# A finer cost model for the instruction order, a split z chain, TensorE flips and more GLU tiles in the FFT stage

## The chip, the cores and the metric

The kernel runs on one core of one Trainium2 chip. The metric is the device time of one execution in microseconds (us), the median of several. A run counts as slow when it is over 1.5% above the fastest run of the same kernel; fast runs are compared with fast runs. The engines are named as in the profile: PE is TensorE (PEld its weight loads), DVE is VectorE, ACT is ScalarE, POOL is GpSimd, SP is the sync engine, which here only issues transfers.

## The reference

The kernel computes a gated block and all its gradients: one output and nine gradients. S = 2048, D = 512, F = 1376, bf16.

```python
# cut: inputs, random numbers and casts are left out
def _A_ref(q, k, v, shift_k, ssm_k, ssm_D):        # q is xn
    k_shift = ...                                   # causal 4-tap filter of k along the sequence
    kv = k_shift * v
    # causal convolution along the sequence by FFTs of length 2 S:
    y = irfft(rfft(pad(kv)) * rfft(pad(ssm_k)))[:S]
    y = y + kv * ssm_D
    return q * y

def _B_ref(x, w_gate, w_up, w_down):                # the GLU
    h = sigmoid(x @ w_gate) * (x @ w_up)
    return h @ w_down

x = A_q
xn = layernorm(x)
s = _A_ref(xn, A_k, A_v, A_shift_k, A_ssm_k, A_ssm_D)
g = silu(_B_ref(xn, B_w_gate, B_w_up, B_w_down))
out = x + s * g
# the kernel returns out and the vector-Jacobian product with grad_out for nine inputs
```

## The kernel before

The FFTs are matmuls with constant matrices. Four stages follow each other: the start (loads, constants), the FFT stage (forward convolution, beside it the forward GLU of eight of the sixteen tiles, of which five are spilled to DRAM), stage B (GLU backward tile by tile, and the forward of the other tiles), and stage C (backward FFT and weight gradients).

The program does not issue its instructions in the order in which it is written. It records them with their dependences, and a scheduler, with a model of each instruction's cost, simulates the engines and puts the instructions of each engine in the order of that simulation. So a wrong cost in the model is a wrong order on the chip. The parts that matter here:

```python
def cost(self, alt):                       # (time on the engine, time to the result)
    if eng == "scalar":
        c = 0.085 + n / 1200
        return c, c + 0.11
    ...                                    # other engines
# cut: in the simulation, when op (started at t, engine occupied for occ, result at fin) is placed
    o = ops[s]                             # an op that depends on it
    r = t + occ if (e == "tensor" and o.alts[0][0] == "tensor") or (e == o.alts[0][0] \
        and len(o.alts) == 1 and not op.dma) else fin + 0.05
    o.ready = max(o.ready, r)              # same engine: ready as soon as the engine is free
```

```python
FA = [12, 10, 8, 6, 4, 0, 1, 2]            # tiles whose forward runs in the FFT stage

def z_gen(i):                              # down projection and gates of tile i, in stage B
    nc.vector.tensor_tensor(s_out, xn, y2, ALU.mult)
    nc.vector.tensor_tensor(dgate, goj, s_out, ALU.mult)
    for fb in range(NFB):
        nc.tensor.matmul(psZ[:], hT[:, fb, :], wd[:, fb, :], ...)
        if fb == 5:
            yield 6 * 512
    # sigmoid on ScalarE, then a chain of dependent VectorE products up to dzA[:, i, :]
    ...
    yield 5 * 512
    # the rest of the chain

def stepB():
    for i in range(NJ):
        ...                                # f: forward of tile i+3, d: dh, x: dx of tile i
        yield from take(z, 9)              # all of z of tile i+1, before most of d
        ...
        yield from take(d, 9); yield from take(f, 9); yield from take(x, 9)

def flip_dma(Qg, Qf):                      # stage C: transposes by transfers on the sync queue
    for c in range(2):
        nc.sync.dma_start_transpose(Qf[:, c], Qg[:, c].rearrange("p g j e -> p (g j e)"))
# stage C, in the gradient of the 4-tap filter:
    nc.vector.memset(dks[96:P, NJ:NJ + 3, :], 0.0)
```

Of the kernel before, what the change touches and what calls it, by code (L numbers as in the profile page):

```python
# [30 lines left out]
FA = [12, 10, 8, 6, 4, 0, 1, 2]  # L31
# [121 lines left out]
class Op:  # L153
    __slots__ = ("n", "alts", "deps", "succ", "wait", "ready", "dma", "tiles", "done", "fin", "eng", "soft")
# [12 lines left out]
class Rec:  # L167
# [64 lines left out]
    def add(self, alts):  # L232
# [37 lines left out]
        op.dma = "dma" in meth  # L270
        self.ops.append(op)
# [8 lines left out]
    def cost(self, alt):  # L280
# [7 lines left out]
        if eng == "scalar":  # L288
            c = 0.085 + n / 1200
            return c, c + 0.11  # L290
        if eng == "vector":
            aps = [v for v in list(a) + list(k.values()) if isinstance(v, (PT, bass.AP))]
            big = [v for v in aps if self.size(v) >= n / 2]
            ps = any(isinstance(v, PT) for v in big)
            wide = any(esize(v.ap.dtype if isinstance(v, PT) else v.dtype) == 4 for v in big)
            rate = 960
            if meth in ("tensor_copy", "tensor_scalar", "tensor_single_scalar", "tensor_scalar_add", "memset"):
                rate = 1920 if (wide and not ps) or (ps and not wide) else 960 if ps else 3840
            elif meth == "tensor_tensor" and not ps and not wide:
                rate = 1920  # L300
            if meth == "bn_stats":
                n = self.size(a[1])
            c = 0.065 + n / rate
            return c, c + 0.09
        if "alu" in meth or meth == "tensor_tensor":
            return 0.3, 1.5
# [27 lines left out]
    def order(self):  # L334
# [30 lines left out]
        seq = []  # L365

        def push(op):
            if len(op.alts) > 1:
                either.append(op)
            else:  # L370
                heapq.heappush(soon[op.alts[0][0]], (op.ready, op.n))
# [13 lines left out]
        while ndone < len(ops):  # L385
# [58 lines left out]
            ndone += 1  # L444
            for v in op.tiles:
# [12 lines left out]
            for s in op.succ:  # L458
# [7 lines left out]
                r = t + occ if (e == "tensor" and o.alts[0][0] == "tensor") or (e == o.alts[0][0] and len(o.alts) == 1 and not op.dma) else fin + 0.05  # L466
# [42 lines left out]
def gen_fft_consts(nc, ar, negpi, Cf, BD, R):  # L509
# [8 lines left out]
    a = tmp([16], i32)  # L518
    nc.gpsimd.iota(a, pattern=[[1, 16]], base=0, channel_multiplier=16)
    b = tmp([128], i32)  # L520
    nc.gpsimd.iota(b, pattern=[[2, 128]], base=1, channel_multiplier=0)
# [50 lines left out]
def kernel_impl(ctx, tc, A_q, A_k, A_v, A_shift_k, A_ssm_k, A_ssm_D, B_x, B_w_gate, B_w_up, B_w_down,  # L572
# [97 lines left out]
    def f_gen(i):  # L670
# [3 lines left out]
        xnT = xnT_r.next()  # L674
        nc.evac(xnT, pt[:], 512)
        yield 512
        n = POS[i]
        if n + 3 < NJ:
            f_x(SEQ[n + 3])
        sigT, hT = sig_r.next(), h_r.next()  # L680
        T[i]["sig"], T[i]["h"] = sigT, hT
        for pi, (f0, nb) in enumerate(FBS):
# [11 lines left out]
            nc.vector.tensor_tensor(hT[:, f0:f0 + nb, :], pu[:, 0:nb, :], sigT[:, f0:f0 + nb, :], ALU.mult)  # L694
            if pi == 1 and n + 1 < NJ:
                f_ln(SEQ[n + 1])
            yield nb * 1024
# [50 lines left out]

    skr_r = Ring(ar, [D * 4])
    ones_r = Ring(ar, [P])  # L750
    skr, ones1 = skr_r.ap[0:1, :], ones_r.ap[0:1, :]
    nc.sync.dma_start(skr, A_shift_k.rearrange("(o d) t -> o (d t)", o=1))
    for i in SEQ[:3]:
# [3 lines left out]
    def ld_w(f0, f1):  # L757
        for w, src in ((wg, B_w_gate), (wu, B_w_up)):
            nc.sync.dma_start(w[:, :, f0:f1], src[:, f0:f1].rearrange("(db p) f -> p db f", p=P))
    ld_w(0, 512)  # L760
    ld_k(0)
    ld_KT(0)
    ld_w(512, 1024)
    ld_w(1024, F)
    ld_v(0)
    nc.scalar.dma_start(Dcol_b, A_ssm_D.rearrange("(cg p) -> p cg", p=P))
    stS_r.append(Ring(ar, [FP]))
# [9 lines left out]
    for db in range(4):  # L777
        pb = ps_mm([512])
        nc.tensor.matmul(pb[:], ones1, skr[:, db * 512:(db + 1) * 512], start=True, stop=True)
        nc.scalar.copy(skb[:, :, db * 128:(db + 1) * 128], pb[:].rearrange("p (d t) -> p t d", t=4))  # L780
    nc.gpsimd.memset(wg[:, :, F:FP], 0.0)
    nc.gpsimd.memset(wu[:, :, F:FP], 0.0)
    make_identity(nc, ident)
    f_ln(SEQ[0])
    gen_fft_consts(nc, ar, negpi, Cf, BD, R)
# [39 lines left out]

    def flip_dma(Qg, Qf):
        for c in range(2):
            nc.sync.dma_start_transpose(Qf[:, c], Qg[:, c].rearrange("p g j e -> p (g j e)"))
# [40 lines left out]
    def strK():  # L869
        for cg in range(NG):  # L870
            KT = stA.pop(("KT", cg))
            nc.gpsimd.tensor_tensor(out=KT[:, 0:1], in0=KT[:, 0:1], in1=Dcol_b[:, cg:cg + 1], op=ALU.add)
# [80 lines left out]
    run_streams([(gG, len(FA) * 11776, 0.1, 0.97), (strK(), 4 * 10240, 0.0, 0.7), (strV(), 4 * 16384, 0.0, 0.8),  # L953
# [24 lines left out]
    dg_r, du_r = Ring(ar, [NFB, 128], n=2), Ring(ar, [NFB, 128], n=2)  # L978

# [29 lines left out]
    def z_gen(i):  # L1009
# [5 lines left out]
        nc.vector.tensor_tensor(s_out, xn, y2, ALU.mult)  # L1015
        nc.vector.tensor_tensor(dgate, goj, s_out, ALU.mult)
# [9 lines left out]
        nc.scalar.activation(t2, sigz, ACT.Identity, bias=1.0, scale=-1.0)  # L1026
        nc.vector.tensor_tensor(t2, gate, t2, ALU.mult)
        nc.vector.tensor_tensor(t2, t2, sigz, ALU.add)
        nc.vector.tensor_tensor(dzA[:, i, :], dgate, t2, ALU.mult)
        yield 5 * 512  # L1030
# [56 lines left out]
    def stepB():  # L1087
        yield from z_gen(0)
        for i in range(NJ):
# [11 lines left out]
            yield from take(f, 1)  # L1101
            run_pend(2)
            yield from take(z, 9)
            if i == NJ - 2:
                flags.add("z15")
# [10 lines left out]
            yield from take(f, 9)  # L1116
            run_pend(2)
            yield from take(x, 9)
            if i + LAG == NJ - 1:
# [60 lines left out]
    def frontC():  # L1180
        for cg in range(NG):
# [5 lines left out]
            flip_dma(Qg, Qf)  # L1187
# [14 lines left out]
    def backC():  # L1202
        for cg in range(NG):
# [33 lines left out]
            nc.vector.memset(dks[96:P, NJ:NJ + 3, :], 0.0)  # L1237
# [92 lines left out]
    live = run_streams([(dw[0], dw[1] - dw[4], 0.0, 1.0), (frontC(), 4 * 4096, -0.05, 0.5),  # L1330
# [67 lines left out]
```

## Time and profile before

| | before |
|---|---|
| timed runs | 604.84 us median of 3 (603.37 to 610.57) |
| profiled run | 597.06 us, span 595.3 us |
| TensorE busy | 540.4 us, 91% |
| sum of its matmuls back to back | 521.4 us |

The last row is the floor that I use below. Unbroken runs of matmuls start 55.8 ns (128 columns) and 215.8 ns (512 columns) apart; I put N/2.4 GHz + 2.5 ns on each of the 5261 matmuls, of which every weight load is in the trace. The time from the first matmul to the last (by the starts of their weight loads) less this floor is what I call waits of TensorE: idle time and half-clock time together, 67.1 us before. A half-clock spell is a stretch in which the clock record shows half the full clock.

The prediction shows the main views of this kernel. Two more lines of its page are needed for comparison: the granted clock of TensorE in 40 slices (in tenths, 9 is full), and the shares of the engines in the chain of waits that ended last.

```profile
PEclk9989999999999999999999999989999999999998
PE 33%; DVE 23%; DMA 18%; issue 17%; ACT 4%; POOL 4%; POOLq 0%; DVEq 0%; ACTq 0%
```

The clock drops in three slices. By the clock record these are the spells at 39.1 and 394.1 us and a fourth one at 592.1 us, which begins after the last matmul has ended (589.8 us) and costs nothing; the spell at 489.7 us falls on the border of two slices and does not show. TensorE has only a third of the chain; 18% is transfers and 23% VectorE. The next view is the timeline of VectorE in stage B (start, duration, then engine, operation and shapes), the statistics of one layer norm tile:

```profile
210.43 0.69 DVE L479 BATCH_NORM_STATS2 slab<-slab 128x6 f32<-128x512 bf16 x1
211.16 0.18 DVE L479 BATCH_NORM_AGGREGATE slab<-slab 128x2 f32<-128x6 f32 x1
211.37 0.15 DVE L479 TENSOR_SCALAR slab<-slab 128x1 f32<-128x1 f32 x1
```

Each step needs the one before, and each starts only after the record of the one before has ended: 210.43 + 0.69 = 211.12, start 211.16. I counted all neighbours on VectorE in this trace. 277 start 20 to 60 ns after the end of their predecessor's record, and 274 of these wait on VectorE's own semaphore; 500 start before that end, 83 ns in the median. In the products of 128x512 bf16, the two kinds show as starts 0.456 us (80 times) and 0.336 us (216 times) apart. A dependent neighbour costs 0.12 us more.

### The profile page before, as it was taken

Reading aid. Unit: us, or ns where it says so; the run is one execution under the profiler, and the core shown is the slowest. Engines: PE = TensorE matmul, PEld = TensorE weight load, DVE = VectorE, ACT = ScalarE, POOL = GpSimd, SP = SyncE. Lnnn points to the kernel's source line nnn. Section 1 sums busy time; section 2 is a strip of 40 time slices with the busy share of each in tenths; the row PEclk is TensorE's granted clock in tenths of the full one; section 3 lists DMA queues with packets and bytes.
Section 4 is the critical chain, followed back from the end, with each engine's and each line's share of the span. In section 5 each row is a group of like instructions: output and inputs, shape, how many; then the busy total and the mean of one; then the engine's idle time right before and its main releaser. Section 6 shows DMA issues by size and latency. Waiting matters only on the chain.

```text
span 595.3 us, 12849 instructions
## 1 busy us (share of the span) xinstructions
PE 540.4 (91%) x5197; PEld 372.0 (62%) x5261; DVE 436.8 (73%) x874; ACT 327.2 (55%) x437; POOL 151.0 (25%) x258
## 2 busy tenths in 40 slices
PE   4878899999989889899889989969999989999986
PEld 3866678787876556566667656534665645665534
DVE  7699998683878887889878789422859688479350
ACT  7879999797853434354334334224646655444411
POOL 2332242422011312222112111310323152340211
PEclk9989999999999999999999999989999999999998
DMA  8976888665217676989876799999899979985561
GB/s 228 276 197 187 272 210 219 203 212 152 89 53 198 173 210 152 242 165 239 195 223 183 174 209 284 216 195 294 228 229 283 217 245 283 217 261 194 150 185 34
DMA packets 143367, 121.64 MB, mean 204 GB/s; under 512 B 91508, under 2 KB 124106, under 8 KB 143307
## 3 DMA queue, kind: packets, MB, share of 16 engines
q1 hardware_dynamic: 126362, 67.03, 47.2%
q0 software_dynamic: 16416, 53.78, 30.3%
q8 instruction: 41, 0.67, 0.5%
q14 instruction: 20, 0.16, 0.1%
q10 hardware_dynamic: 528, 0.00, 0.0%
HBM read 52.79 MB, written 46.11 MB: 166 GB/s over the span
## 4 chain that ended last, share of the span: by engine, by line
PE 33%; DVE 23%; DMA 18%; issue 17%; ACT 4%; POOL 4%; POOLq 0%; DVEq 0%; ACTq 0%
PE psum L479 33%; DVE slab L479 23%; DMA slab<-slab 8%; ACT slab L479 4%; DMA out_dram<-slab 2%; DMA KK_d<-slab 2%; DMA slab<-in_grad_out_dram 2%; POOL slab L479 1%; DMA ksh_d<-slab 1%; DMA hF_d<-slab 1%; POOL out_dram L479 1%; POOL KK_d L479 1%; DMA slab<-in_A_k_dram 1%; POOL sF_d L479 0%; POOLq L479 0%
## 5 line engine op out<-in xcount | busy, mean ns | idle before, releaser
L479 PE MATMUL psum<-slab 128*128 128x128 bf16 (+4 forms) x5197 | 540.4, 263 | 49.4 <-ACT slab L479 25.5
L479 PEld LDWEIGHTS <-slab 128*128 128x128 bf16 (+2 forms) x5261 | 372.0, 99 | 217.5 <-issue 36.4
L479 DVE TENSOR_TENSOR slab<-slab 128x512 bf16<-128x512 bf16 (+5 forms) x551 | 301.4, 587 | 39.9 <-ACT slab L479 23.2
L479 ACT CAST slab<-psum 128x1024 bf16<-128x1024 f32 (+4 forms) x245 | 201.5, 855 | 159.7 <-PE psum L479 135.3
L479 POOL DMA_DIRECT2D out_dram<-slab x75 | 44.1, 591 | 219.7 <-DVE slab L479 141.0
L479 ACT COPY slab<-psum 128x1024 bf16<-128x1024 bf16 (+2 forms) x74 | 60.5, 839 | 27.9 <-PE psum L479 27.5
L479 DVE TENSOR_TENSOR slab<-psum,slab 128x512 bf16<-128x512 f32 (+2 forms) x68 | 44.4, 655 | 27.0 <-PE psum L479 15.1
L479 ACT ACTIVATE slab<-psum 128x512 bf16<-128x512 f32 (+1 forms) x64 | 37.3, 584 | 48.8 <-PE psum L479 46.1
L479 ACT ACTIVATE slab<-slab 128x512 bf16<-128x512 bf16 (+3 forms) x51 | 40.2, 802 | 25.6 <-DVE slab L479 24.9
L479 POOL DMA_DIRECT2D KK_d<-slab x32 | 20.2, 637 | 48.2 <-ACT slab L479 39.3
L479 DVE SCALAR_TENSOR_TENSOR slab<-slab 128x1 f32<-128x1 f32 (+3 forms) x64 | 28.0, 438 | 4.0 <-ACT slab L479 2.8
L479 DVE CAST slab<-psum 128x1024 bf16<-128x1024 f32 (+1 forms) x12 | 14.1, 1177 | 19.4 <-PE psum L479 18.8
L479 POOL DMA_DIRECT2D slab<-in_A_q_dram x29 | 16.5, 570 | 37.5 <-ACT slab L479 21.7
L479 DVE COPY slab<-psum 128x1024 bf16<-128x1024 bf16 (+2 forms) x26 | 16.1, 632 | 12.8 <-PE psum L479 12.6
L479 DVE SCALAR_TENSOR_TENSOR slab<-psum,slab 128x512 f32<-128x512 f32 x16 | 11.0, 690 | 18.9 <-PE psum L479 18.8
L479 POOL DMA_DIRECT2D slab<-KK_d x16 | 11.6, 723 | 29.2 <-DVE slab L479 27.1
L479 DVE TENSOR_SCALAR slab<-slab 128x1 f32<-128x1 f32 (+8 forms) x49 | 16.8, 358 | 1.7 <-ACT slab L479 1.0
L479 POOL TENSOR_TENSOR slab<-slab 128x1 f32<-128x1 f32 (+1 forms) x20 | 12.9, 646 | 12.3 <-DVE slab L479 10.7
L479 POOL DMA_DIRECT2D slab<-in_grad_out_dram x16 | 9.3, 579 | 16.7 <-DMA out_dram<-slab 15.3
L479 DVE BATCH_NORM_STATS2 slab<-slab 128x6 f32<-128x512 bf16 x16 | 11.0, 688 | 0.6 <-DMA slab<-in_A_q_dram 0.5
L479 POOL DMA_DIRECT2D slab<-slab x8 | 4.6, 572 | 24.7 <-DVE slab L479 16.5
L479 POOL DMA_DIRECT2D slab<-in_A_k_dram x12 | 10.2, 851 | 1.5 <-issue 0.7
(22 smaller groups left out, 39.3 us busy)
## 6 DMA issues: line engine op xcount, KB each, us to landing
KK_d<-slab POOLq DMA_DIRECT2D x32, 256.0 KB, 3.9
slab<-KK_d POOLq DMA_DIRECT2D x16, 512.0 KB, 7.5
out_dram<-slab POOLq DMA_DIRECT2D x58, 128.0 KB, 4.0
hS_d<-slab SPq DMA_DIRECT2D x16, 352.0 KB, 3.0
dgS_d<-slab SPq DMA_DIRECT2D x16, 352.0 KB, 3.3
duS_d<-slab SPq DMA_DIRECT2D x16, 352.0 KB, 3.6
slab<-hS_d SPq DMA_DIRECT2D x8, 512.0 KB, 5.0
slab<-dgS_d SPq DMA_DIRECT2D x8, 512.0 KB, 8.1
```

The lines of the kernel that those rows point to most:

```text
L479: getattr(getattr(self.nc, eng), meth)(*[place(v) for v in a], **{x: place(v) for x, v in k.items()})
```

## The change

It has these parts: a finer model for the order; the z chain of the next tile split, so that its last part stands after the matmuls of d and x of this tile; two more buffers for it; the flips of dy in stage C as TensorE transposes; layer norm two tiles ahead and the transposed tile (xnT) one tile ahead; another load order; ten forward tiles in the FFT stage instead of eight, seven of them spilled instead of five; and one memset from VectorE to GpSimd. (Also one small addition from GpSimd to VectorE, and new weights of the streams.) The core of the diff:

```diff
-FA = [12, 10, 8, 6, 4, 0, 1, 2]
+LATE = 0.25
+AHEAD = 500
+FA = [14, 13, 11, 9, 7, 5, 4, 0, 1, 2]
@@ model: durations
-            c = 0.085 + n / 1200
-            return c, c + 0.11
+            c = 0.05 + n / 1200 + (0.2 if not isinstance(k.get("scale", 1.0), float) else 0.0)
+            return c, c + 0.12
... (VectorE 0.065 to 0.07; reductions by their input; GpSimd scalar operations)
@@ model: transfers that are far ahead of TensorE are held back
+            if op.dma and op.n > front[0] + AHEAD:
+                held.append(op)
@@ model: latency
-                r = t + occ if (e == "tensor" and o.alts[0][0] == "tensor") or (... same engine ...) else fin + 0.05
+                same = e == o.alts[0][0] and len(o.alts) == 1 and not op.dma
+                r = t + occ + (0.0 if e == "tensor" else 0.12) if same else fin + 0.05 + (LATE * (fin - t) if op.dma else 0.0)
@@ z_gen: three parts instead of two
-        nc.vector.tensor_tensor(s_out, xn, y2, ALU.mult)
-        nc.vector.tensor_tensor(dgate, goj, s_out, ALU.mult)
...
+        yield 5 * 512
+        nc.vector.tensor_tensor(s_out, xn, y2, ALU.mult)
         nc.vector.tensor_tensor(t2, gate, t2, ALU.mult)
+        nc.vector.tensor_tensor(dgate, goj, s_out, ALU.mult)
...
-        yield 5 * 512
+        yield 64
@@ stepB
-            yield from take(z, 9)
+            yield from take(z, 2)
...
             yield from take(f, 9)
+            yield from take(z, 1)
             run_pend(2)
             yield from take(x, 9)
+            yield from take(z, 9)
@@ stage C
-            flip_dma(Qg, Qf)
+            yield from flip(Qg, Qf)
...
-            nc.vector.memset(dks[96:P, NJ:NJ + 3, :], 0.0)
+            nc.gpsimd.memset(dks[96:P, NJ:NJ + 3, :], 0.0)
... (layer norm and xnT ahead, load order, buffers: left out)
```

## The prediction

> **What bounds the kernel now.** I read the page first. Its first part says that TensorE (PE) holds the span:
>
> ```profile
> span 595.3 us, 12849 instructions
> PE 540.4 (91%) x5197; PEld 372.0 (62%) x5261; DVE 436.8 (73%) x874; ACT 327.2 (55%) x437; POOL 151.0 (25%) x258
> ```
>
> So TensorE is idle for 595.3 - 540.4 = 54.9 us, and busy time can shrink only if work is removed. Next, the waits of TensorE: whom it waits for in its idle time.
>
> ```profile
> PE psum L479 <- ACT slab L479: 25.5, 28, 5.1
> PE psum L479 <- DVE slab L479: 16.8, 21, 4.4
> ...
> PE psum L479 <- DMA slab<-slab: 0.6, 1, 0.6
> ```
>
> 42.3 us are waits for the two engines that empty PSUM and prepare operands; transfers are almost never what TensorE waits for directly. Third, the busy times in stretches that I cut by the program's stages, found from what is stored and loaded when (spills of h and KK_d stores in the first part, dgS_d stores in the middle, KK_d loads and output stores at the end): start, FFT stage, stage B (GLU backward), stage C (backward FFT and weight gradients).
>
> ```profile
> core 0: us, PE busy (x) PEld busy (x) DVE busy (x) ACT busy (x) POOL busy (x), PEclk, DMA share, GB/s
> 0.00:28.00 28.00, 17.75 (x229) 15.47 (x230) 19.81 (x53) 23.63 (x27) 8.33 (x25) 1.00 0.92 261
> 28.00:166.00 138.00, 127.31 (x1630) 105.47 (x1647) 113.42 (x182) 121.22 (x145) 40.51 (x67) 0.99 0.67 189
> 166.00:398.00 232.00, 211.02 (x2076) 141.31 (x2097) 185.28 (x452) 90.14 (x156) 48.33 (x85) 0.99 0.81 196
> 398.00:596.00 198.00, 184.32 (x1270) 109.71 (x1290) 118.30 (x188) 92.21 (x110) 53.83 (x83) 0.98 0.80 216
> ```
>
> Length less PE busy gives the idle time of each stage: 10.3, 10.7, 21.0 and 13.7 us (0.7 of the last lies past the end). In the FFT stage ScalarE (ACT) is busy 88% and VectorE (DVE) 82%, so three engines are near full there. In stage B DVE has 80% and ACT 39%.
>
> Last, the timeline at two stalls of stage B. The first repeats whenever a GLU forward tile runs inside this stage:
>
> ```profile
> 215.65 1.05 ACT L479 CAST slab<-psum 128x512 bf16<-128x512 f32 x2
> 216.59 0.59 ACT L479 COPY slab<-psum 128x512 bf16<-128x512 bf16 x1
> 217.24 0.55 PE L479 MATMUL psum<-slab 128*128 128x128 bf16 x7 [1.48 <-ACT slab L479]
> ```
>
> TensorE has just transposed a normalised tile; the copy to SBUF (bf16 from bf16 PSUM, so a transpose) stands behind two other evictions on ACT, and the first gate matmul waits 1.48 us. The second is the border of B and C:
>
> ```profile
> 393.18 0.22 DVE L479 MEMSET slab<- 32x192 uint32 x1 [11.07 <-DMA slab<-slab]
> ...
> 394.18 2.29 PE L479 MATMUL psum<-slab 128*128 128x512 bf16 x5 [4.36 <-DVE slab L479]
> 394.18 0.10 PEld L479 LDWEIGHTS <-slab 128*128 128x128 bf16 x1 [4.48 <-issue]
> 394.56 0.15 PEld L479 LDWEIGHTS <-slab 128*128 128x128 bf16 x1 [0.28 <-issue]
> 394.99 0.15 PEld L479 LDWEIGHTS <-slab 128*128 128x128 bf16 x1 [0.28 <-issue]
> ```
>
> A DVE memset of a stage C buffer waits 11.07 us for a transfer (transposing reads of the memory it reuses), the last tile's arithmetic queues behind it, and TensorE waits 4.36 us for the PSUM bank that this arithmetic reads. Then the weight loads come 0.43 us apart, twice the usual spacing.
>
> **What the skill says.** "TensorE: Matmul & The Clock Gate", section "Wait — 56ns, not 53.3ns?", gives N/2.4 GHz + about 2.5 ns between starts, 55.6 and 215.7 ns for 128 and 512 columns. The trace agrees: unbroken runs start 55.8 and 215.8 ns apart. Part 1 of the page gives half clock after an idle window of about 3.4 us. The trace's clock record has three such spells inside the span, 3.41 us each, at 39.1, 394.1 and 489.7 us; a spell costs up to 1.7 us. Its "Engine queue depths" says that ACT and DVE are strict FIFO; the memset shows it. Its "Part 4: PE-mode transpose" says that a transpose lands in PSUM and needs a copy, about 275 ns each in a kernel; here a 128-column record lasts 221 ns on average, but their starts are 55.8 ns apart, so I cost 55.8.
>
> **The change, part by part.**
>
> *dy flips on TensorE.* Four groups, each 2 x 16 transposes: 128 x 55.8 ns = 7.1 us more on TensorE, all in stage C where it is 93% busy, so all on the path. 16 evictions at 1.04 us (row ACT COPY 128x1024) = 16.6 us of ACT, which has 106 us free in C: beside. Eight transfers of 512 KB leave the sync queue, and with them waits such as 372.88 to 403 us in the chain, which holds "DMA slab<-slab" pieces of 20.2 and 9.5 us. But TensorE fills stage C with weight-gradient matmuls (14.92 of 15 us busy from 405 to 420), so the earlier start of the backward FFT is worth little by itself.
>
> *Two more tiles in the FFT stage.* A tile is 92 matmuls of 128 columns = 5.13 us. So 10.3 us of TensorE work move from B to the FFT stage; the sum is unchanged. ACT takes per tile two sigmoids of 512 (0.61) and one of 384 (0.51), the xnT copy (0.59) and the LN activation (0.73) = 3.05 us; DVE takes 2 x 0.69 + 0.55 + LN 1.2 = 3.1 us. Two spills and reloads more are 2 x 2 x 352 KB each way, 2.8 MB, some 10 us of transfer at 270 GB/s (an estimate from the rates in the stretches), beside.
>
> *xnT and LN ahead.* Stalls over 1 us in B: about 1.5, 1.7, 1.7, 1.7, 1.2, 1.5, 1.2, 1.0, 2.0 and the 4.4 at the border, some 18 of 21 us. Four stand directly behind an xnT copy; the others are a PSUM bank or operand that waits for ACT or DVE while those stand behind something that came too early. Taking xnT a tile ahead removes the four, 6.5 us.
>
> *z chain split and finer model.* z of the next tile now starts before the matmuls of d and x of this one, so its ten DVE steps have about 7 us (44 x 55.8 ns + 22 x 215.8 ns) to hide in. With the finer order I give them half of the remaining 7 us: 3.5.
>
> *Memset to GpSimd.* The DVE queue is free at the border: 4.4 us and the half-clock spell (up to 1.7): 6.
>
> *Load order and start.* One x tile before the weights, K's filter before k, LN before the FFT constants: first tile matmul at 9.16 us now. I give 3 of the 10.3 us.
>
> Sum by stage. Start and FFT stage: 166 now; + 10.3 work, - 3 start, - 3 idle filled by the extra tiles (10.7 us is there, but ACT at 88% limits it) = 170. B: 232 - 10.3 - 6.5 - 3.5 - 6 = 205.7; I add 3 for the ten tiles without forward work (before eight), where DVE's 11.3 us per tile exceeds TensorE's 9.8 = 209. C: 197.3 + 7.1 - 2 (fewer waits for transfers) = 202. Total 581. Taking the reverse way, the idle time falls from 55 to about 32 and busy time rises by 5 (7 less a half-clock spell): 577. I take 579, a ratio of 0.973. The timed median is 604.84, above the profile's 595.3, so 604.84 x 0.973 = 588; I lean to 586, as the reordering touches more small waits than I counted.
>
> **Rivals.** (1) *The FFT stage takes it all back.* Before: ACT + DVE of start and FFT stage 278 us over two engines, 139 of 166 us. After: 278 + 12.3 = 290, 145 us, and TensorE 155. If packing stays as it is, the stage grows by the whole 10.3, and the start gives nothing: +6, about 592. For it: 88% ACT. Against: late in the stage (135 to 150 us) DVE has 6 and ACT 10.7 of 15 us, and the new weights of the streams put the tiles earlier, where TensorE has 11 to 13 of 15.
> (2) *DVE becomes the bound of B.* DVE 185 - 2 x 3.1 = 179 us in B against TensorE's 201. At the 80% of now that is 224 us, so B would shrink by only 8: total near 594 profiled, 604 timed, no gain. Against: DVE's own idle time in B is mostly waiting for TensorE and ACT.
> (3) *The flips cost more than they free.* If C was hidden behind weight gradients anyway, +7 and no return: 2 us more than I count.
> (4) *All idle of B vanishes.* Then B is 201, total 570, timed 575.
>
> **Range and chances.** Point 586. Rivals (1) and (2) in part give 598; (4) with a better FFT stage gives 572. Timed runs scatter between 603.4 and 610.6. Faster by over 2% (below 592.7): 0.73; within: 0.23; slower: 0.04.
>
> **What would show it.** PE busy near 545; idle near 32. No 1.5 us stall behind a 512-wide bf16 copy in B. No 11 us DVE memset wait, and one half-clock spell fewer. First tile matmul near 7 us. End of the FFT stage near 170, of B near 379. 48 instead of 56 DMA transposes, ACT COPY 128x1024 up by about 16. It is wrong if the FFT stage ends past 178, if DVE is over 92% in B, or if the memset now blocks GpSimd's queue of transfers so that stage C waits for loads.

## The result

The changed kernel takes 566.41 us (median of 4 runs, 564.35 to 569.34, all fast); the kernel before takes 605.57 us beside it (4 runs). The ratio is 0.9346, 95% interval 0.9268 to 0.9425. A ratio is taken within one job, from runs of the same rounds, so it is not quite the ratio of the medians. The result lies below the predicted range of 572 to 598 us: faster, as expected, but by about twice the predicted gain.

From the page of the changed kernel, and its waits of TensorE (engine, what it wrote, whom it waited for: us in all, times, longest):

```profile
span 562.7 us, 13136 instructions
PE 536.1 (95%) x5330; PEld 378.2 (67%) x5389; DVE 420.8 (75%) x873; ACT 343.1 (61%) x454; POOL 155.2 (28%) x266
```

```profile
PE psum L493 <- ACT slab L493: 13.0, 14, 5.2
...
PE psum L493 <- DVE slab L493: 2.2, 4, 1.0
```

Waits for ScalarE fall from 25.5 to 13.0 us, and waits for VectorE from 16.8 us in 21 pieces to 2.2 us in 4. The window view by stage, cut as in the prediction some 5 to 10 us behind the ends of the stages that the table of waits below gives:

```profile
core 0: us, PE busy (x) PEld busy (x) DVE busy (x) ACT busy (x) POOL busy (x), PEclk, DMA share, GB/s
0.00:28.00 28.00, 19.27 (x223) 15.86 (x225) 18.55 (x49) 22.91 (x26) 6.45 (x20) 1.00 0.87 246
28.00:176.00 148.00, 138.95 (x1912) 120.04 (x1926) 121.96 (x209) 130.87 (x165) 47.18 (x80) 1.00 0.72 204
176.00:372.00 196.00, 193.70 (x1847) 127.79 (x1864) 167.18 (x432) 85.42 (x144) 47.30 (x84) 1.00 0.98 229
372.00:564.00 192.00, 184.15 (x1358) 114.54 (x1379) 113.10 (x185) 103.87 (x122) 54.24 (x84) 1.00 0.66 200
```

In stage B TensorE is idle for 2.3 of 196 us, where it was idle for 21.0 of 232 us. DVE has 85% there and is not the bound. Most of the idle time left is in the first two rows. The clock and the chain answer to the two lines shown of before:

```profile
PEclk9999999999999999999999999999999999999999
PE 64%; DVE 14%; issue 9%; ACT 9%; POOL 2%; DMA 1%; POOLq 0%; DVEq 0%; ACTq 0%
```

All three half-clock spells that lay between matmuls are gone, and the share of transfers in the chain falls from 18% to 1%. VectorE in stage B, where the same three statistics instructions run (208 to 212 us):

```profile
209.04 0.68 DVE L493 BATCH_NORM_STATS2 slab<-slab 128x6 f32<-128x512 bf16 x1
209.65 0.67 DVE L493 SCALAR_TENSOR_TENSOR slab<-psum,slab 128x512 f32<-128x512 f32 x1
...
211.19 0.17 DVE L493 BATCH_NORM_AGGREGATE slab<-slab 128x2 f32<-128x6 f32 x1
211.31 0.16 DVE L493 SCALAR_TENSOR_TENSOR slab<-slab 128x2 f32<-128x2 f32 x1
211.40 0.15 DVE L493 TENSOR_SCALAR slab<-slab 128x1 f32<-128x1 f32 x1
```

Work of other chains now stands between the dependent steps, and each instruction starts before the record in front of it has ended (209.65 against 209.04 + 0.68 = 209.72). Dependent neighbours on VectorE fall from 277 to 98. At 0.12 us each that is 21 us; VectorE's busy time, with nearly the same instructions, falls by 16.0 us (436.8 to 420.8).

The waits by stage, by the floor method. The cuts are at 28 us, at the last matmul of the FFT streams, at the last matmul of dx in stage B, and at the end:

| | floor | start | FFT stage (ends) | stage B (ends) | stage C | all waits |
|---|---|---|---|---|---|---|
| before | 521.4 | 13.5 | 17.2 (160.4) | 19.1 (386.4) | 17.3 | 67.1 |
| after | 528.5 | 11.9 | 12.7 (170.8) | 2.0 (362.0) | 0.9 | 27.5 |

The floor grows by 7.1 us, waits fall by 39.6, and the span by 32.6. The timed medians differ by more, 39.2 us: the profiled run of before (597.06 us) was some 8 us faster than its median, that of after (564.47) some 2 us.

### The profile page after: what moved, and what is told of

Same layout as the page of the kernel before. It is cut to its first block, busy times and chain, and to the rows that moved or that the text cites. A ratio compares the mean times of both kernels' runs of the same rounds, so it can differ in the third digit from the quotient of the medians.

```text
span 562.7 us, 13136 instructions
## 1 busy us (share of the span) xinstructions
PE 536.1 (95%) x5330; PEld 378.2 (67%) x5389; DVE 420.8 (75%) x873; ACT 343.1 (61%) x454; POOL 155.2 (28%) x266
## 4 chain that ended last, share of the span: by engine, by line
PE 64%; DVE 14%; issue 9%; ACT 9%; POOL 2%; DMA 1%; POOLq 0%; DVEq 0%; ACTq 0%
PE psum L493 64%; DVE slab L493 14%; ACT slab L493 9%; POOL out_dram L493 1%; DMA ksh_d<-slab 1%; POOL slab L493 0%; POOLq L1420 0%; POOLq L493 0%; DVEq L493 0%; ACTq L493 0%; POOLq L1409 0%
## 5 line engine op out<-in xcount | busy, mean ns | idle before, releaser
L493 PE MATMUL psum<-slab 128*128 128x128 bf16 (+4 forms) x5330 | 536.1, 261 | 21.3 <-ACT slab L493 13.0
L493 PEld LDWEIGHTS <-slab 128*128 128x128 bf16 (+1 forms) x5389 | 378.2, 99 | 178.8 <-issue 13.3
L493 DVE TENSOR_TENSOR slab<-slab 128x512 bf16<-128x512 bf16 (+3 forms) x555 | 291.5, 579 | 38.4 <-ACT slab L493 25.3
L493 ACT CAST slab<-psum 128x1024 bf16<-128x1024 f32 (+3 forms) x242 | 200.1, 857 | 98.9 <-PE psum L493 92.7
L493 ACT COPY slab<-psum 128x1024 bf16<-128x1024 bf16 (+2 forms) x94 | 79.4, 887 | 86.9 <-PE psum L493 86.3
L493 DVE SCALAR_TENSOR_TENSOR slab<-slab 128x1 f32<-128x1 f32 (+3 forms) x64 | 28.0, 437 | 13.8 <-ACT slab L493 12.6
L493 DVE COPY slab<-psum 128x1024 bf16<-128x1024 bf16 (+2 forms) x22 | 14.0, 646 | 19.9 <-PE psum L493 18.4
L493 DVE CAST slab<-psum 128x1024 bf16<-128x1024 f32 (+1 forms) x15 | 17.4, 1161 | 9.0 <-PE psum L493 8.9
L493 DVE TENSOR_SCALAR slab<-slab 128x1 f32<-128x1 f32 (+8 forms) x49 | 16.6, 355 | 2.0 <-ACT slab L493 1.8
L493 POOL TENSOR_TENSOR slab<-slab 128x1 f32<-128x1 f32 x16 | 11.4, 712 | 18.3 <-DVE slab L493 18.1
L493 POOL DMA_DIRECT2D slab<-slab x8 | 4.5, 566 | 26.0 <-issue 17.1
L493 DVE BATCH_NORM_STATS2 slab<-slab 128x6 f32<-128x512 bf16 x16 | 10.8, 683 | 0.0
```

Source lines behind the costliest of these rows:

```text
L493: getattr(getattr(self.nc, eng), meth)(*[place(v) for v in a], **{x: place(v) for x, v in k.items()})
```

## The experiments

Each run was made beside the kernel before on the same chip. That kernel's medians in the five jobs were 602.32, 604.07, 600.29, 607.22 and 602.34 us, slow runs included; its fast runs alone give 602.32, 604.06, 598.75, 601.18 and 596.58 us. In the fourth job (after_no012, after_noLate, before_LZT, before_ZT) four of the seven runs of the kernel before count as slow, and the ratios come out only with these left in: against its three fast runs (mean 600.99 us) I get 0.974, 0.954, 0.977 and 1.019. The changed kernel itself ran only in the first job; times are compared across jobs. Four versions that change little (after_noMem, after_mc, after_noG, after_11) took 566.4 to 567.3 us on three chips, so its 566.41 us carries over. The runs of one kernel lie up to some 6 us apart, except where the table says more, so differences below that are not settled by a median. Waits are from the profiled run, by stage as above; for the kernels without the new flips the floor is 521.4 us, for the others 528.5; the profiled run of after_noM is a slow one. "Dependent" is the number of dependent neighbours on VectorE, where I counted it.

| kernel | timed median (range), us | ratio to before (95%) | waits start / FFT / B / C | dependent |
|---|---|---|---|---|
| before | 605.57 (603.37-610.57) | 1 | 13.5 / 17.2 / 19.1 / 17.3 | 277 |
| after | 566.41 (564.35-569.34) | 0.935 (0.927-0.943) | 11.9 / 12.7 / 2.0 / 0.9 | 98 |
| after_noM | 619.11 (605.29-627.57) | none | 15.9 / 29.0 / 16.5 / 29.2 | 256 |
| after_noZ | 592.76 (589.32-597.53) | 0.984 (0.977-0.992) | 12.1 / 12.6 / 28.0 / 1.0 | 99 |
| after_noT | 572.47 (569.52-574.53) | 0.949 (0.943-0.956) | 12.5 / 12.5 / 1.9 / 16.6 | 103 |
| before_M | 611.36 (609.39-614.89) | 1.015 (1.009-1.021) | 14.9 / 12.7 / 22.0 / 25.4 | 89 |
| after_noX | 577.10 (569.47-578.65) | 0.951 (0.938-0.964) | 11.4 / 17.2 / 2.9 / 1.2 | |
| after_noMem | 566.66 (564.91-570.86) | 0.942 (0.934-0.949) | 12.7 / 12.6 / 1.9 / 0.9 | |
| after_noF | 571.61 (569.21-576.64) | 0.951 (0.941-0.961) | 12.4 / 15.9 / 1.4 / 4.3 | |
| after_noHold | 568.38 (565.50-573.26) | 0.944 (0.936-0.953) | 12.4 / 14.4 / 1.4 / 2.8 | |
| after_noConst | 568.99 (565.67-571.13) | 0.950 (0.945-0.956) | 13.1 / 9.5 / 2.8 / 6.4 | 99 |
| after_noLat | 589.84 (588.87-591.32) | 0.985 (0.981-0.990) | 15.4 / 17.8 / 13.1 / 7.5 | 263 |
| before_MZT | 571.37 (568.90-573.70) | 0.955 (0.950-0.960) | 14.5 / 13.8 / 2.7 / 0.9 | 115 |
| after_mc | 567.18 (565.11-570.90) | 0.948 (0.943-0.954) | 10.6 / 12.9 / 1.9 / 8.5 | |
| after_no012 | 585.08 (583.67-586.67) | 0.967 (0.959-0.975) | 12.8 / 20.2 / 10.8 / 2.9 | 264 |
| after_noLate | 578.01 (569.15-580.60) | 0.946 (0.933-0.959) | 12.0 / 12.5 / 2.0 / 5.6 | 92 |
| before_LZT | 586.97 (585.73-587.95) | 0.969 (0.963-0.975) | 14.3 / 13.6 / 14.0 / 8.6 | 111 |
| before_ZT | 611.95 (611.08-613.77) | 1.011 (1.004-1.017) | 13.5 / 17.5 / 16.4 / 27.0 | 264 |
| after_noG | 567.27 (565.69-570.87) | 0.951 (0.942-0.960) | 11.5 / 12.0 / 4.8 / 1.4 | |
| after_11 | 566.43 (562.01-572.12) | 0.952 (0.939-0.965) | 11.5 / 10.7 / 1.9 / 1.1 | |

### One large part undone or done alone

**after_noM.** All changes of the model undone (durations, hold-back, latency), the rest of the change kept.

```diff
-            c = 0.05 + n / 1200 + (0.2 if ... else 0.0)
+            c = 0.085 + n / 1200
... and the other lines of the model, as in the kernel before
```

> The changed kernel with the old cost model for the order (old constants, no holding back of transfers, no added latency between instructions of one engine), all else as changed. Theory A, the finer model places the work and took away most waits of TensorE in stages B and C (34 of the 40 us gained): time near 590, 20 us or more of TensorE waits back in B and C. Theory B, the restructuring (xnT ahead, z split, flips, memset) took them away and the model only trims: under 575, waits in B and C together under 8 us.

Three of its four runs, the profiled one among them, count as slow, so there is no ratio, and the 619 us mixes states. Its one fast run took 605.29 us. That alone says enough: with everything else of the change in place and the old model, the kernel is about where it was before. Theory B fails; theory A has the place right (stages B and C) and the size too small.

**after_noZ.** The z chain is issued as before.

```diff
-            yield from take(z, 2)
+            yield from take(z, 9)
... z_gen in two parts, its first two products ahead of the matmuls
```

> The changed kernel with the z chain as before (one piece, all of it ahead of the matmuls of d and x, s_out and dgate first). Theory B (structure): the z chain stands in VectorE's queue ahead of what TensorE needs, 8 to 12 us of waits come back in stage B, time near 576. Theory A (model): the order is found anyway, at most 3 us, under 570.

It is 26.3 us slower by the medians, and all of it is in stage B, whose waits go from 2.0 to 28.0 us. The timeline of TensorE there, with the idle time before a piece in brackets:

```profile
247.62 1.05 PE L493 MATMUL psum<-slab 128*128 128x128 bf16 x16 [0.93 <-ACT slab L493]
249.36 1.28 PE L493 MATMUL psum<-slab 128*128 128x128 bf16 x20 [0.69 <-ACT slab L493]
251.08 23.08 PE L493 MATMUL psum<-slab 128*128 128x128 bf16 x215 [0.45 <-ACT slab L493]
275.09 1.05 PE L493 MATMUL psum<-slab 128*128 128x128 bf16 x16 [0.93 <-ACT slab L493]
```

The same three gaps, 0.93, 0.69 and 0.45 us, return every 27.5 us, once per round of the order. They are small, and none looks like a 26 us problem; over the stage, with some longer ones, they are one. In all, TensorE waits in stage B 11.9 us for ScalarE in 18 pieces and 7.9 us for VectorE in 4, against 0.8 us each in the changed kernel; two half-clock spells come on top. Each of the three short gaps waits for a ScalarE instruction on a result that TensorE has only just made (in the first, at 247.00 us, it stands behind two activations of z); the two longest, 2.89 and 2.69 us, end with a 128x512 product of VectorE. That the unsplit chain leaves TensorE no other matmuls at these places is my reading. Dependent neighbours stay at 99, so the model's part still works. Theory B had the direction, with a third to a half of the size; theory A fails.

**after_noT.** The flips of dy are transposing transfers again.

```diff
-            yield from flip(Qg, Qf)
+            flip_dma(Qg, Qf)
```

> The changed kernel with dy flipped by DMA transposes again: 7.1 us less matmul time. My prediction's reading (stage C is full of weight-gradient matmuls, the flips only cost): 559 to 562, faster than the changed kernel by 4 to 7 us. Rival, the transposes hold up the sync queue and with it the loads and the start of the backward FFT: C gets 7 us or more of waits back, time 566 to 572.

The floor falls by 7.1 us as it must, but the waits of stage C rise from 0.9 to 16.6: the profiled span is 8.7 us longer, the median 6.1. The timeline of TensorE in stage C:

```profile
412.72 27.44 PE L493 MATMUL psum<-slab 128*128 128x512 bf16 x202 [2.80 <-DMA slab<-slab]
444.57 1.67 PE L493 MATMUL psum<-slab 128*128 128x256 bf16 x6 [4.41 <-DVE slab L493]
```

"DMA slab<-slab" at 412.72 us is one of the flips: issued at 396.57 us, it landed at 412.68. Only this gap waits for a flip directly. At 444.57 us TensorE waits for VectorE work that had itself waited 4.96 us for a transfer of GpSimd's queue, and a third gap, 2.90 us before 471.52, stands behind ScalarE, which had waited 4.03 us for an output store. That these two come from the later start of the backward FFT is my reading. The clock record has half-clock spells of 3.41 us at 413.3, 444.0 and 471.3 us, within 0.6 us of the ends of these three gaps. So the 7.1 us of transposes buy back about 16 us of waits, of which up to 5.1 us are half clock. My prediction's reading (559 to 562 us) fails; its rival holds, though the time is just above its 566 to 572 us and only one gap is the queue's directly.

**before_M.** The kernel before with the finer model alone.

```diff
... only the lines of the model of the change
```

> The kernel before with only the finer cost model. Theory A: 580 to 585 (20 us or more of waits in B and C gone). Theory B: 598 to 606, waits in B still over 18 us.

It is 1.5% slower than before; theory A fails, and the time lies above theory B's range too. Dependent neighbours fall to 89, so the rule does what it is for; the waits of stage B stay (22.0 us) and those of stage C grow to 25.4. Its waits of TensorE say on what:

```profile
PE psum L492 <- ACT slab L492: 25.5, 32, 5.1
PE psum L492 <- DMA slab<-slab: 14.3, 2, 7.5
PE psum L492 <- DVE slab L492: 10.7, 6, 3.8
```

Two waits of about 7 us, before 411.83 and 539.94 us, are for the flips by transfer. The order is better packed, and the two things that the program itself forces, the unsplit z chain and the flips on the sync queue, stay. (That the waits of stage B are owed to the z chain is inferred: before_MZT, with the split, has 2.7 us there.)

### The smaller parts

**after_noX.** Layer norm and xnT are made just in time, as before.

```diff
-    def f_xnT(i): ...
... xnT back in f_gen, f_ln(SEQ[n + 1]) back
```

> The changed kernel with xnT and the layer norm just in time again (one tile ahead for LN, xnT at the start of its own tile), z split and the rest kept. My prediction gave this part 6.5 us in stage B (four stalls behind an xnT copy, now six tiles run there). If it stands: 6 to 10 us of waits back in B, time 573 to 577. Rival, with z out of the way the copy comes in time anyway: under 3 us, under 570.

The profile shows 5.2 us more waits, of which 4.5 are in the FFT stage (12.7 to 17.2) and 0.9 in stage B. Only two of its four timed runs count as fast (569.47 and 576.13 us), so the time says no more than "some us". The expected 6 to 10 us of waits in stage B did not come.

**after_noMem.** The memset stays on VectorE.

```diff
-            nc.gpsimd.memset(dks[96:P, NJ:NJ + 3, :], 0.0)
+            nc.vector.memset(dks[96:P, NJ:NJ + 3, :], 0.0)
```

> The changed kernel with the memset of the stage C buffer on VectorE again. My prediction gave it 6 us at the border (4.4 us wait and a half-clock spell). If it stands: TensorE waits 4 us or more at the end of B and the time is 571 to 573. Rival: the wait came from the DMA transposes of dy in front of the sync queue and from the late z chain; with those gone the memset finds its memory free, under 1 us, 565 to 568.

Nothing changes: 566.66 us. The memset at the border of stages B and C, in the timeline of VectorE:

```profile
358.96 0.22 DVE L493 MEMSET slab<- 32x192 uint32 x1 [0.55 <-DMA slab<-slab]
```

It waits 0.55 us where it waited 11.07 us before. With the rest of the change its wait has gone already, so it no longer matters on which engine it stands. The rival's time holds; its reason, the flips in front of the sync queue, does not, as shown below.

**after_noF.** Eight forward tiles in the FFT stage, as before.

```diff
-FA = [14, 13, 11, 9, 7, 5, 4, 0, 1, 2]
+FA = [12, 10, 8, 6, 4, 0, 1, 2]
```

> The changed kernel with eight forward tiles in the FFT stage instead of ten (old list, five spilled). The sum of matmul time stays. If the FFT stage had idle TensorE time for the two tiles (my prediction gave 3 us): 568 to 572, FFT stage ending near 163. Rival: the two tiles only move their 10.3 us and B has as little waiting either way: within 2 us of the changed kernel.

5.2 us slower by the medians and 6.2 us longer in the profile. Stage B has no more waits than after (1.4 us); the FFT stage has 3.2 more and stage C 3.4 more. In the FFT stage the two tiles fill idle time; why stage C differs I did not trace.

### Which line of the model

**after_noHold.** Transfers are not held back.

```diff
-AHEAD = 500
+AHEAD = 1000000
```

> The changed kernel with the cost model's new constants but without holding transfers back until the matmul front is within 500 operations of them. The old model as a whole cost 60 us. If the hold is what counts (transfers placed far too early block their queue): 580 or more. Rival, the constants and the 0.12 us between instructions count: 565 to 570.

Within the scatter of the runs (568.38 us; 3.5 us more waits), as the rival said. The 60 us in this expectation is from slow runs of after_noM.

**after_noConst.** The old durations with the new rules.

```diff
-            c = 0.05 + n / 1200 + (0.2 if ... else 0.0)
+            c = 0.085 + n / 1200
... and the VectorE, reduction and GpSimd durations as before
```

> The changed kernel, with the durations in the model of the order (ScalarE, VectorE, GpSimd) as they were before; the hold-back of transfers and the added latency between dependent instructions of one engine stay. The whole old model cost 619 us against 566; holding back alone is worth under 4 us. Theory A (the durations matter: the model thought a ScalarE eviction 0.035 us too long and an activation with a per-row scale 0.2 us too short, and so chose the wrong engine for evictions): over 595 us, with waits back in the FFT stage and in stage C. Theory B (what matters is the latency between dependent instructions of one engine and the late landing of transfers): 566 to 575 us, and the run without the latency is the slow one.

568.99 us: theory A fails. The 619 us in this expectation is the median of after_noM; its fast run is the better figure.

**after_noLat.** The new durations with the old rules of latency and landing.

```diff
-                r = t + occ + (0.0 if e == "tensor" else 0.12) if same else fin + 0.05 + (LATE * (fin - t) if op.dma else 0.0)
+                r = t + occ if (... same engine ...) else fin + 0.05
```

> The changed kernel, with the old rule for dependent instructions of one engine (the next may start when the first has freed the engine, no 0.12 us after it) and for transfers (landing as computed, not a quarter later). Theory B: over 595 us, because the model packs chains of VectorE instructions, such as the ten steps of z, too tightly and lets other work come too late. Theory A: 566 to 575 us. Both slow by some 20 us each would mean that the two belong together.

589.84 us: theory B holds, though just below the 595 us that I had set for it. Dependent neighbours are back at 263 and waits are back in all stages.

**after_no012** and **after_noLate** take the two rules apart.

```diff
-                r = t + occ + (0.0 if e == "tensor" else 0.12) if same else ...
+                r = t + occ + 0.0 if same else ...
```

> The changed kernel with the 0.12 us between dependent instructions of one engine taken out of the model; the later landing of transfers stays. In the trace of the changed kernel a 512-wide VectorE product starts 0.33 us after the one before if it does not use its result and 0.45 us after if it does; such dependent neighbours number 277 on VectorE in the kernel before, 98 in the changed one, 263 in the run without both rules. Theory B1 (the 0.12 us alone makes the order interleave chains): 585 to 592 us, dependent neighbours back over 230. Rival B2 (the late landing carries it): 566 to 572 us.

```diff
-LATE = 0.25
+LATE = 0.0
```

> The changed kernel with transfers taken to land as computed (not a quarter later); the 0.12 us stays. B1: 564 to 572 us, dependent neighbours on VectorE near 98. B2: 585 us or more.

Without the 0.12 us the time is 585.08 us with 264 dependent neighbours. TensorE then waits for VectorE again, 16.0 us where it was 2.2:

```profile
PE psum L493 <- DVE slab L493: 16.0, 16, 2.5
...
PE psum L493 <- ACT slab L493: 12.1, 12, 4.7
```

Without the late landing the profile is 4.6 us longer, all of it in stage C, and the two fast runs took 569.15 and 577.28 us; the median of 578.01 holds two slow runs. So B1 holds for the larger part, and its range for after_noLate fails by the median: the late landing is worth a few us too, how many is not settled. The rule acts on ScalarE and GpSimd as well, and no run takes VectorE alone. But the neighbours on ScalarE that start 20 to 60 ns after the end of the one before and wait on its own semaphore are 15 before, 16 after and 16 without the rule: what the rule changes in the traces is VectorE.

### How much is enough

**before_MZT.** The kernel before with the finer model, the z split with its buffers, and the flips on TensorE.

```diff
... only these three parts of the change
```

> The kernel before with only three parts of the change: the finer model of the order, the z chain split with its extra buffers, and the flips of dy on TensorE. Theory C (these three carry the gain; the rest are a few us each): 572 to 583 us, a ratio of 0.945 to 0.965, the waits of TensorE in stage B under 8 us and in stage C under 4. Rival D (the gain is that of the whole restructuring, as the finer model alone made the kernel before 1.5% slower): over 590 us.

571.37 us. Theory C holds: the time lies a little below its range of 572 to 583 us, the ratio of 0.9546 and the waits inside theirs. In the same job two versions of the changed kernel with one small edit took 568.99 (after_noConst) and 567.18 us (after_mc), and the changed kernel 566.41 in its own job, so all the other parts together are worth some 2 to 5 us.

**before_ZT.** The same without the model.

```diff
... only the z split with its buffers, and the flips
```

> The kernel before with the z chain split, its buffers and the flips, and the old model unchanged. If the program's order alone did it: under 580 us. If the split only pays when the model knows that dependent instructions follow each other more slowly: 590 us or more, dependent neighbours on VectorE near 270.

611.95 us, 1.1% slower than before (1.9% against the fast runs alone), not faster in any case. The largest single wait of TensorE is 14.37 us in stage C, for a ScalarE eviction. The timelines of ScalarE and of the sync queue show what stood in front of it:

```profile
411.90 1.93 ACT L479 COPY slab<-psum 128x1024 bf16<-128x1024 bf16 x2 [15.31 <-DMA duS_d<-slab]
```

```profile
373.10 29.66 SPq L479 DMA_TRANSPOSE slab<-slab  x2
402.86 0.87 SPq L479 DMA_DIRECT2D dgS_d<-slab  x1
405.48 0.33 SPq L479 DMA_DIRECT2D duS_d<-slab  x1
```

The eviction waits for a spill (duS_d) that must have read the memory it writes, and the spill stands in the sync queue behind two transposing transfers whose issue takes 29.66 us, where that of the others mostly takes 1.4 to 3 us. These are transfers that remain in the changed kernel, not the flips. That an order made with transfers landing too early walks into this is my reading of it; before_MZT, with the whole model, has 0.9 us of waits in stage C.

**before_LZT.** As before_MZT, but of the model only the 0.12 us rule.

```diff
+                same = e == o.alts[0][0] and len(o.alts) == 1 and not op.dma
+                r = t + occ + (0.0 if e == "tensor" else 0.12) if same else fin + 0.05
```

> The kernel before with the 0.12 us rule as the only change of the model, the z chain split with its buffers, and the flips on TensorE. If these few lines carry nearly all: 568 to 576 us, beside 571.37 with the whole finer model. If durations, late landing and holding back matter too: over 580 us.

586.97 us, between the two outcomes that I had named as exclusive. The one rule takes 25 of the 40.6 us between before_ZT and before_MZT (two jobs, so some 2 us are open); the other 15.6 belong to the durations, the late landing and the hold-back in this program, in stages B and C (14.0 and 8.6 us of waits). In the changed kernel each of these three alone was worth a few us at most, so they stand in for each other, or need the rest; I did not take them apart here.

**after_noG.** Without the second set of buffers.

```diff
-    go_r.extend(Ring(ar, [D]))
-    xq2_r.extend(Ring(ar, [D]))
```

> The changed kernel without the second set of buffers for grad_out and x of stage B (the z chain stays split). If part of what I put down to the split is owed to these buffers: over 572 us, with waits of TensorE in stage B over 6 us. If the split alone carries it: 564 to 570 us.

567.27 us: the split alone carries it, not the buffers. Waits of stage B rise from 2.0 to 4.8 us in the profile, too little to show in the time.

### Two attempts at a faster version

**after_mc.** One temporary per half of the FFT constants.

```diff
-    mc = tmp([2, 16, 128], i32)
+    mcs = [tmp([2, 8, 128], i32), tmp([2, 8, 128], i32)]
... each half uses its own
```

> The changed kernel, with one temporary for each half of the FFT constants instead of one that both halves share. In the trace of the changed kernel a VectorE instruction at 9.31 us waits 1.80 us for ScalarE to read the first half. If this is on the path of the start: 1 to 2 us less (564.5 us), waits of the start from 11.9 to about 10. Rival: the start is bound by the loads, and nothing changes (within 1 us).

The waits of the start fall by 1.3 us, as expected, and the time does not (567.18 us). The waits of stage C went from 0.9 to 8.5 us in the profile although nothing was edited there. The order is one global computation, and a small edit early in it can move things late in it; but the profiled run is also the slowest of the four (570.90 us, the others 565.11 to 567.41), so part of the 8.5 us may be that run's own.

**after_11.** Eleven forward tiles in the FFT stage.

```diff
-FA = [14, 13, 11, 9, 7, 5, 4, 0, 1, 2]
+FA = [14, 13, 12, 11, 9, 7, 5, 4, 0, 1, 2]
```

> The changed kernel with eleven forward tiles in the FFT stage and eight spilled (tile 12 added to the list). The work moves, none is added, but stage B now has only 2.0 us of waits left to save and ScalarE is busy 88% in the FFT stage: 565 to 570 us, the FFT stage ending near 176 us, no better than ten. If moving tiles still paid as in the step from eight to ten (571.61 to 566.41): 563 to 565 us.

566.43 us (one of the four runs counts as slow; 565.60 without it), no difference that the runs could show, although its profile is the shortest of all (560.2 us, waits 25.2). No version that beats the changed kernel was found.

## Why the prediction was wrong

The direction was right. Of the terms, two were far too small (the z split with the model, and what the flips give back), and two had a wrong mechanism (the memset, and where xnT helps). The prediction's sum of the profile, 581 us by stages (I took 579), missed 562.7 by 18.3 us. By the floor method the terms come out as follows. The wait at 394 us, to which I gave 6 us in stage B, lies past the last matmul of B, so I count it in C here. The work of the flips is the floor's own figure; the trace agrees, as 128-column matmuls of stage C start 56 ns apart in the median and all waits of that stage are 0.9 us.

| term | predicted, us | measured, us |
|---|---|---|
| work of the flips | +7.1 | +7.1 |
| start | -3 | -1.6 |
| idle filled in the FFT stage | -3 | -4.5 |
| waits of stage B (-6.5 xnT, -3.5 z and model, +3) | -7 | -17.1 |
| waits of stage C (-6 memset, -2 fewer transfer waits) | -8 | -16.4 |

- **The step that failed most: "With the finer order I give them half of the remaining 7 us: 3.5."** I priced the z split and the model as one small rest. Undone one at a time, the split is worth 26 us and the model about 39 by its single fast run. I had the split's effect right in kind (time to hide the chain in), but I counted only gaps over 1 us, "some 18 of 21 us". The gaps that the unsplit chain causes in the new order are mostly below that. Even all of the 7 us, and without the 3 us that I added for tiles with no forward work and that did not come, would have made 13.5 of the 17.1 us. And I did not price the model at all, though the trace of before held its main figure: 277 dependent neighbours on VectorE at 0.12 us more each, 33 us of VectorE. after_no012 shows that this one rule is worth 18.7 us in the changed kernel.
- **The second: "the earlier start of the backward FFT is worth little by itself", with 2 us for it.** The cost of the flips was exact, 7.1 us. Their return is near 16 us of waits (after_noT): three gaps with a half-clock spell each, of which one waits for a flip itself. I had looked at one stretch that was full (405 to 420 us) and took all of stage C to be so. And of the two pieces of the chain that I put down to the flips, 20.2 and 9.5 us, the first is not one of them (see the memset). Rival (3), that the flips cost more than they free, is refuted by after_noT.
- **"Taking xnT a tile ahead removes the four, 6.5 us"**: in the changed kernel it is worth some 5 us by the profile, and nearly all of it in the FFT stage, not in B. In B the better order hides the xnT copy in either form.
- **The memset, 6 us**: moving it to GpSimd is worth nothing in the changed kernel. The wait that I saw was real, 11.07 us, but what the memset waited for came late; I took the waiter for the cause. It was not a flip either: the transfer was issued at 372.88 us, took 20.2 us to land, and feeds the spill to dgS_d at 400.15; the first flip was issued at 393.74, after the wait had ended. Transfers of its kind remain in the changed kernel. Why its like lands in time there stays open.
- **The FFT stage** was close: predicted end near 170, measured 170.8, and rival (1) did not come. That is partly luck: the start gave 1.4 us less than predicted and the filled idle time 1.5 us more. **The start** was wrong: the first matmul of the first GLU tile came at 12.20 us (its weight load at 11.24), not near 7, against 9.16 before; only transposes of K's filter came earlier, at 9.34. The tile's layer norm waits in VectorE's queue behind an instruction of the FFT constants, which itself waits 1.80 us for ScalarE's sine.
- **Rival (2)** did not come: VectorE is busy 85% in B. **Rival (4)**, that all idle time of B vanishes, came nearest: 2.0 us of waits are left there. It said 570, timed 575; by the prediction's own stages (170, 201 and 202 us) it is 573, timed some 582, so part of its nearness is a slip. The rest of the way is stage C. (Rival 2 has a slip too: its stages add up to 596, not 594.) I had given this rival only the low end of the range.
- **The checks.** TensorE busy 536.1, not 545: busy records contain half-clock time, which went, up to 5.1 us in three spells; the rest of the difference I did not trace. Idle 562.7 - 536.1 = 26.6 us, predicted 32. Three half-clock spells fewer, not one. 48 transposing transfers, as predicted, and ScalarE copies of 128x1024 from 41 to 59, predicted +16.
- **Half-clock spells.** The prediction tied them to an idle window of about 3.4 us. The traces say something else: no idle gap near the spells at 39.1 and 489.7 us was longer than 2.24 us. Cut each of the 20 traces into windows of 3.41 us on the grid on which its spells begin: at full clock, 51 windows end with the start of a spell, and in each of them TensorE was idle for 2.00 us or more in sum by its records; in the other 3184 it was idle for 1.98 us at most. So several short gaps close together can cost a spell, and a single one of 2 us can do it.

**Why so much came at once.** The single removals add up to far more than the 39 us gained, so the parts depend on each other. Two by two, in timed medians:

| timed median, us (ratio to before in the same job) | program as before | z split and flips |
|---|---|---|
| old model | 605.57 (1) | 611.95 (1.011) |
| finer model | 611.36 (1.015) | 571.37 (0.955) |

Each half alone gains nothing (1 to 2% slower), both together make the kernel 4.5% faster. The traces show how each is blocked without the other. With the model alone, TensorE still waits for the unsplit z chain and for the flips by transfer (before_M). With the split and the flips alone, the order strings dependent VectorE instructions together (264 neighbours), and one long wait stands behind transfers that land late (before_ZT). An estimate that takes one part at a time against the kernel before, as mine did, cannot see this.

**What stays open:** how the remaining 15.6 us of the model in before_LZT divide; and how much of the start could be gained, as after_mc freed 1.3 us there and the time did not follow; and why the transposing transfers at the border of B and C take so long, 20.2 us from issue to landing before, and 29.66 us for the issue of two in before_ZT.

## What to carry to other kernels

Where a program's order comes from a cost model, measure in the trace how far apart dependent and independent neighbours of one engine start, and put that difference into the model first: here 0.12 us per pair was worth more than all corrections of durations. Moving a transpose from a transfer queue to a busy TensorE can pay although TensorE is the bound, if TensorE's gaps stand behind that queue. And test the parts of a change two by two before you call one of them worthless: here each half alone gained nothing.

## What the Trainium skill lacked or had wrong

- "VectorE: DVE Perf Modes", section "The DRAIN you can't avoid", says that "the next op does not start until the 8-stage pipe empties" and, of its test, that "the semaphore costs nothing extra here", adding that an op that is not held starts earlier. It has no figure for the difference. Here an instruction that waits for the result of the one in front starts about 35 ns after that record's end, and one that does not, 80 ns before it: 0.456 against 0.336 us from start to start for 128x512 bf16 products. A wait on VectorE's own semaphore that an older instruction has already satisfied is free: 229 of the overlapping neighbours in the changed kernel have one.
- "TensorE: Matmul & The Clock Gate", "Part 4: PE-mode transpose", gives about 275 ns for a transpose in a kernel. As cost to TensorE that is too much here: starts of 128-column matmuls in stage C, the 128 new transposes among them, are 56 ns apart in the median, and the prediction that used 55.8 ns was right on this term.
- "DMA: Bandwidth & Descriptors", section "Latency and other measured facts", gives transposing transfers a bandwidth, 261 GB/s in one case, which would be an estimated 1.4 us for the 352 KB of one that stays in this kernel. What counted here was the time in the queue: the issue of two transposing transfers took 29.66 us of the sync queue in before_ZT, and the spill behind them held up ScalarE for 15.31 us. The spread of the issue time, from 1.3 us up, is what a plan needs.
- No page says how much of a window TensorE may idle before the clock is halved (this belongs to "TensorE: Matmul & The Clock Gate"). In the 20 traces 2.00 us of idle time in a window of 3.41 us brought a spell and 1.98 us did not.
